# Two chunks of a state-space scan per visit to TensorE, between the products of an expert layer

## The chip, the cores and the metric

The kernel runs on one core of a Trainium2 chip. A core has five engines that run side by side and meet at semaphores: TensorE (PE in the profile, its weight loads PEld), VectorE (DVE), ScalarE (ACT), GpSimd (POOL) and SyncE (SP), which here only issues DMAs. The metric is the device time of one execution in microseconds. Before the change the median of three runs is 651.06 us (650.8 to 651.61).

## The reference

Two parts, the second of which reads the output of the first. The first is a Mamba-2 layer (4 sequences, 8 heads, 768 tokens, head size 32, state size 16), here cut to one chunk:

```python
cum = np.cumsum(la, axis=-1)                     # la: log of the decays a
L = np.exp(cum[..., :, None] - cum[..., None, :]) * causal
M = np.einsum('bhin,bhjn->bhij', Cc, Bc) * L
y = M @ xc + np.einsum('bhin,bhnd->bhid', Cc, state) * np.exp(cum)[..., None]
state = decay_full * state + sum_j(Bc_j, xc_j, decay_from_j)
```

The result does not depend on the length of a chunk; the kernel takes 128 tokens. The second part is a sum over four experts on the 3072 tokens, each with 256 inputs and 1024 hidden units:

```python
p = domain_probs / (domain_probs.sum(-1, keepdims=True) + 1e-09)
for e in range(4):
    out += p[:, e:e + 1] * (np.maximum(x @ w1[e], 0.0) @ w2[e])
```

Everything is float32.

## The kernel before

**Blocks and steps.** There are 24 chunks of 128 tokens. Four of them, the k-th chunk of each of the four sequences, make block k of 512 tokens (`CPB` is 4, `NBLK` is 6). A block goes through the experts in 8 steps (`SPB`), one for each half of each expert's hidden units, so there are 48 steps; step n is step r = n % 8 of block k = n // 8. Steps 0 and 1 are done in the prologue in the plain way, with 8 products of blocks instead of 7. From step 2 on a loop (L736 to L821) runs.

**A step.** Both products of a step are 2 x 2 block products made with seven multiplications each, of sums and differences. `fmul(n, i)` is multiplication i of the first product (f1 to f7 below), `smul(n - 1, i)` that of the second product of the step before (s1 to s7). Each is two matmuls of 128 x 128 by 256, which in float32 are four instructions of PE. The order on PE in a step is

```
f1 f2 s1 f6 s3 [outputs] f5 f7 s7 s5 f3 f4 s6 s2 [scores] s4
```

The results of f go into two PSUM banks, X (f1, f6, f7, f4) and Y (f2; f5, f3). ACT copies X after f1, f6 and f7 (`snap`, L459). DVE adds such a copy to Y (`total`, L464), applies relu and the gate (`gated`, L474; `gated 21` reads X itself, after f4) and makes four differences `hT1` to `hT4` (`diff`, L481), of which two come at the end of the step and two, in the list `late`, after the first total and gate of the next one. The second product gathers in four PSUM banks, acc0 to acc3, over a block; at the beginning of the next block (r = 0 and 1) `keep`, `combine` and `turned_out` take the result out of them, and `leave` stores it in steps 2 to 5.

**The chunks of the next block** are worked between these products, one at a time. The programs of a chunk c:

- `load_chunk` (L120): tokens `xb` (L106; four buffers), the decays spread over all partitions `ab` (L112; three buffers), and the decays per head `ah` (L118; three buffers), all issued by SP
- `masks` (L355): two ACT instructions that make `ctm`, C with the one or the other half of the heads set to zero
- `decay_part` 0 and 1 (L322): each a scan on DVE over half of the heads, which makes half of `LT`, the decays between all pairs of tokens (L346); after the second, POOL makes the last columns of `MT`, B weighted for the state (L351)
- `decay_part` 2: a scan on DVE, `dec` (L329), and on POOL `cts`, C weighted with it (L332)
- `scores` (L362): products of C and B on PE, four 32-row tiles of the array, one for each quarter of the partitions, each into a PSUM bank of its own; for the chunks in the loop two banks of the pool `att`, X and Y (L369)
- `masked` (L375): four DVE products of these with `LT`, into `MT` (L379)
- `outputs` (L383): on PE the carried state times `cts` (L392, full array), and on top of it `MT` times x in 32-column tiles (L398); ACT copies the y (L404) and the new sum for the state (L407) out of PSUM
- `carry` (L409): three short DVE instructions that update the state of the sequence

`scores` or `outputs` of one or more chunks, between products that use the full array, are called a visit below. The entry of chunk c (masks, scans, scores, masked products) stands in steps r = 0, 2, 4, 6, its exit (outputs) in the step after, its carry in the one after that. For the first block that is fed in the loop, chunk 4 enters in the prologue (L713 to L730).

**What sets the order.** The schedule is written by hand: each engine works its instructions in the order in which the program calls them, and waits are put in where a tile is read, written or its buffer reused. A pool's tile with `bufs=n` takes the buffer of the n-th tile of its tag before it. In the pool `att`, two buffers are the rule; `LT` has one, and each `hT` has two in the pool `ffn`. SP issues its DMAs in order as well: weights of step n + 2, gates, outputs, and the chunk loads. POOL, in the first block, also makes sums of weights (`sum_w1`, `sum_w2`) and stores them.

Of the kernel before, what the change touches and what calls it, by code (L numbers as in the profile page):

```python
# [8 lines left out]
FP32 = mybir.dt.float32  # L9
# [8 lines left out]
def kernel(  # L18
# [9 lines left out]
):  # L28

# [79 lines left out]
    def load_decays(c, queue):  # L109
        if c >= SPREAD:  # L110
            ab = load.tile([P, NH * P], FP32, tag="ab", name="ab")
            nc.sync.dma_start(  # L112
                out=ab, in_=acut_d[real(c)].rearrange(
                    "h s -> (h s)").partition_broadcast(P))
            st.setdefault(c, {})["ab"] = ab
        if c >= CPB:
            ah = st[c]["ah"] = load.tile([HN, P], FP32, tag="ah", name="ah")
            queue.dma_start(out=ah, in_=ac_d[real(c)].unsqueeze(1).to_broadcast([NH, N, P]))  # L118

    def load_chunk(c):  # L120
        load_tokens(c)
        load_decays(c, nc.sync)
# [199 lines left out]
    def decay_part(c, part):  # L322

        s = st[c]
        if part == 2:
            if c >= CPB:

                s["dec"] = dec = att.tile([HN, P], FP32, tag="dec", name="dec")
                nc.vector.tensor_tensor_scan(  # L329
                    out=dec, data0=s["ah"], data1=zeros, initial=1.0, op0=ALU.mult, op1=ALU.add)  # L330
                s["cts"] = cts = att.tile([HN, NT, P], FP32, tag="cts", name="cts")
                nc.gpsimd.tensor_mul(cts, s["ctm"], dec.unsqueeze(1).to_broadcast([HN, NT, P]))  # L332
            return
        half = NH * P // 2
        if part == 0:
            if c >= SPREAD:
                s["a"] = [s["ab"][:, :half], s["ab"][:, half:]]
            LT = att.tile([P, NH * P], FP32, tag="LT", name="LT", bufs=1)
            s["LT"] = LT.rearrange("p (h s) -> p h s", h=NH)

            s["MT"] = att.tile([P, NH, P + N], FP32, tag="MT", name="MT")

        LT, w = s["LT"].rearrange("p h s -> p (h s)"), s["a"][0].shape[1]
        n = half // w
        for i in range(n * part, n * part + n):
            nc.vector.tensor_tensor_scan(  # L346
                out=LT[:, i * w:i * w + w], data0=s["a"][i],
                data1=ident.rearrange("p h s -> p (h s)")[:, :w], initial=0.0,
                op0=ALU.mult, op1=ALU.add)
        if part == 1 and c < NCH - CPB:  # L350
            nc.gpsimd.tensor_mul(  # L351
                s["MT"][:, :, P:], s["xb"][:, OB:OB + HN].rearrange("p (h n) -> p h n", h=NH),
                s["LT"][:, :, P - 1:P].to_broadcast([P, NH, N]))

# [7 lines left out]
    def scores(c, homes):  # L362

        s = st[c]
        s["g"] = []
        for q, (pool, tag) in enumerate(homes):
            k = slice(32 * q, 32 * q + 32)
            g = pool.tile([P, NT, P], FP32, tag=tag, name="g")
            nc.tensor.matmul(  # L369
                out=g.rearrange("p t s -> p (t s)"), lhsT=s["xb"][k, OBT:OBT + P],  # L370
                rhs=s["ctm"][k].rearrange("p t s -> p (t s)"),
                start=True, stop=True, tile_position=(32 * q, 0))
            s["g"].append(g)

    def masked(c, qs):  # L375
        s = st[c]
        for q in qs:
            h = slice(NT * q, NT * q + NT)
            nc.vector.tensor_mul(s["MT"][:, h, 0:P], s["g"][q], s["LT"][:, h])  # L379

    state = {}

    def outputs(c, pool, tag):  # L383

        s = st[c]
        k, i = divmod(c, CPB)
        first = k == 0
        w = P + N if k < NBLK - 1 else P
        xb, MT = s["xb"], s["MT"]
        y = pool.tile([P, NT, P + N], FP32, tag=tag, name="y")  # L390
        if not first:
            nc.tensor.matmul(  # L392
                out=y[:, :, 0:P], lhsT=state[i][1].rearrange("p q d -> p (q d)"),
                rhs=s["cts"], start=True, stop=False, skip_group_check=True)
        for t in range(NT):
            for q in range(NQ):
                h = NQ * t + q
                nc.tensor.matmul(  # L398
                    out=y[32 * q:32 * q + 32, t, 0:w], lhsT=xb[:, h * D:h * D + D],
                    rhs=MT[:, NT * q + t, 0:w], start=(first and t == 0), stop=True,  # L400
                    tile_position=(0, 32 * q), skip_group_check=True)
        if i == 0:
            yT[k] = ffn.tile([P, NT, BLK], FP32, tag="yT", name="yT")
        nc.scalar.copy(out=yT[k][:, :, i * P:i * P + P], in_=y[:, :, 0:P])  # L404
        if w > P:
            s["A"] = att.tile([P, NT, N], FP32, tag="A", name="A", bufs=4)
            nc.scalar.copy(out=s["A"], in_=y[:, :, P:])  # L407
# [70 lines left out]
    def diff(n, o, x, y):  # L478
        h = hid[n]
        h[o] = ffn.tile([P, JJ, HB], FP32, tag="h" + o, name="h" + o)  # L480
# [179 lines left out]
    scores(0, homes)  # L660
# [5 lines left out]
    masked(0, range(NQ))  # L666
    outputs(0, ps_att, "att")
    scores(1, banks)
# [4 lines left out]
    masked(1, range(NQ))  # L673
    outputs(1, ps_att, "att")
    spread(2, (1,))
    sum_w1(0, 0)
    load_decays(3, nc.sync)
# [6 lines left out]
    scores(2, homes)  # L684
# [8 lines left out]
    masked(2, range(NQ))  # L693
    outputs(2, ps_att, "att")

    scores(3, ((ps_s, "acc0"), (ps_s, "acc1"), (ps_s, "acc2"), (ps_att, "att")))
# [7 lines left out]
    masked(3, range(NQ))  # L704
    sum_w2(1, 0)
    plain_gated(1, 1)
    outputs(3, ps_att, "att")
# [5 lines left out]
    masks(4)  # L713
# [7 lines left out]
    decay_part(4, 2)  # L721
# [7 lines left out]
    scores(4, ((ps_att, "att"), (ps_att, "att"), (ps_f, "X"), (ps_f, "Y")))  # L729
    masked(4, (2, 3, 0, 1))  # L730
# [4 lines left out]
    late = []  # L735
    for n in range(PLAIN, NS):  # L736
        k, r = divmod(n, SPB)

        enter, exit = ({2: 1, 4: 2, 6: 3}, {2: 0, 3: 1, 5: 2, 7: 3}) if k == 0 else (
            {0: 0, 2: 1, 4: 2, 6: 3}, {1: 0, 3: 1, 5: 2, 7: 3})  # L740
        c_in, c_out = (CPB * (k + 1) + d[r] if r in d and k < NBLK - 1 else None
                       for d in (enter, exit))
# [15 lines left out]
        if c_in is not None:  # L758
            masks(c_in)
            decay_part(c_in, 0)  # L760
# [8 lines left out]
        if c_out is not None:  # L769
            outputs(c_out, ps_att, "att")  # L770
# [11 lines left out]
        if c_in is not None:  # L782
            decay_part(c_in, 1)
# [6 lines left out]
        if c_out is not None and c_out + 2 < NCH:  # L790
            load_chunk(c_out + 2)
# [7 lines left out]
        smul(n - 1, 6)  # L799
        smul(n - 1, 2)  # L800
        if c_in is not None:
            scores(c_in, ((ps_att, "att"), (ps_att, "att"), (ps_f, "X"), (ps_f, "Y")))
            masked(c_in, (2, 3, 0, 1))
        diff(n, "T3", "22", "12")
        if c_in is not None:
            decay_part(c_in, 2)
# [11 lines left out]
        if PLAIN < n <= CPB:  # L818
            late.append(lambda n=n: carry(n - 1))
        if c_out is not None:  # L820
            late.append(lambda c=c_out: carry(c))  # L821
# [48 lines left out]
```

## Time and profile before

| | |
|---|---|
| median of three runs | 651.06 us |
| the profiled execution | 650.64 us |
| its span, first to last instruction | 648.8 us |
| granted TensorE clock | 0.999 |
| POOL busy up to 105 us of the span (prologue and first block) | 65.9 us |
| POOL busy in the 544 us after | 43.2 us |
| matmuls of L369 (scores) | 192, 17.4 us in all |
| matmuls of L392 and L398 (outputs) | 40 and 384, 11.9 and 16.7 us in all |

The busy time of the table is that of one execution under the profiler. A line of a timeline gives the start from the beginning of the span, the length, the engine, the line of the kernel, the operation with what it writes and reads, how many instructions were merged into it, and in brackets how long the engine stood idle before it and what ended that. "Issue" stands where the engine waited for nothing that the profile shows. A wait line gives the total, the number of times and the longest.

### The profile page before, as it was taken

The page shows a single profiled execution, that of the slowest core. Times are in us where ns is not written, and L with a number is a line of the kernel's source. Part 1 is how long each engine was busy: PE and PEld are TensorE (multiplying, and loading weights), DVE is VectorE, ACT ScalarE, POOL GpSimd, SP SyncE. Part 2 cuts the span into 40 slices and gives each one's busy share as a digit, 9 for nine tenths or more (in the row PEclk, how much of TensorE's full clock was granted, in tenths as well). Part 3 has the DMA queues.
Part 4 walks back from the last instruction along what each step waited for, and adds up shares of the span by engine and source line. Part 5 has one row for each costly group of instructions (what it writes and reads, how often), then busy time and mean ns, then how long its engine had stood idle before and what let it go on. Part 6 is the DMA issues. An engine that isn't in the chain of part 4 may idle for free.

```text
span 648.8 us, 9091 instructions
## 1 busy us (share of the span) xinstructions
PE 643.4 (99%) x3367; PEld 541.9 (84%) x3367; DVE 478.4 (74%) x809; ACT 115.7 (18%) x247; POOL 109.2 (17%) x157
## 2 busy tenths in 40 slices
PE   9999999999999999999999999999999999999997
PEld 5888888888888888888888888888888888888886
DVE  7868878878677797686787867778767667756555
ACT  3011121211211122112121121122111211111110
POOL 4787565020000001000002000000100000100000
PEclk9999999999999999999999999999999999999999
DMA  6987977624678361777742467836185644156001
GB/s 226 331 292 250 341 285 244 228 108 130 200 244 302 124 233 32 241 225 251 242 153 91 131 204 218 323 135 223 38 250 171 241 178 129 60 161 226 1 0 33
DMA packets 95648, 121.61 MB, mean 187 GB/s; under 512 B 28520, under 2 KB 77556, under 8 KB 95604
## 3 DMA queue, kind: packets, MB, share of 16 engines
q1 hardware_dynamic: 92776, 111.20, 52.7%
q0 software_dynamic: 2304, 9.44, 3.6%
q8 instruction: 27, 0.44, 0.3%
q10 hardware_dynamic: 524, 0.39, 0.2%
q14 instruction: 17, 0.14, 0.1%
HBM read 108.16 MB, written 12.83 MB: 186 GB/s over the span
## 4 chain that ended last, share of the span: by engine, by line
PE 99%; DVE 0%; ACT 0%; issue 0%
PE acc L537 43%; PE X L452 24%; PE Y L452 19%; PE g L369 2%; PE y L398 2%; PE acc L518 2%; PE y L392 1%; PE X L501 1%; PE Y L501 1%; PE t L652 1%; PE a L312 1%; PE a L304 0%; PE gp L281 0%; PE turned L588 0%; DVE u L603 0%; DVE o L614 0%
## 5 line engine op out<-in xcount | busy, mean ns | idle before, releaser
L464 DVE TENSOR_TENSOR z<-Y,snap 128x512 f32<-128x512 f32 x138 | 94.7, 686 | 127.3 <-ACT snap L459 81.5
L537 PE MATMUL acc<-hT,wt 128*128 128x256 f32 x736 | 183.2, 382 | 0.0
L459 ACT COPY snap<-X 128x512 f32<-128x512 f32 x138 | 80.8, 586 | 465.8 <-PE X L452 465.8
L537 PEld LDWEIGHTS acc<-hT,wt 128*128 128x128 f32 x736 | 138.5, 190 | 23.7 <-issue 6.0
L452 PE MATMUL X<-yS,wt 128*128 128x256 f32 x552 | 141.8, 379 | 0.0
L537 PE MATMUL acc<-h,wt 128*128 128x256 f32 x552 | 141.6, 379 | 0.0
L452 PEld LDWEIGHTS X<-yS,wt 128*128 128x128 f32 x552 | 105.1, 190 | 14.1
L537 PEld LDWEIGHTS acc<-h,wt 128*128 128x128 f32 x552 | 105.1, 190 | 14.1
L474 DVE SCALAR_TENSOR_TENSOR h<-z,gate 128x512 f32<-128x512 f32 x138 | 97.8, 709 | 3.5 <-PE acc L518 0.4
L452 PE MATMUL Y<-yT,wt 128*128 128x256 f32 x368 | 94.5, 379 | 0.0
L452 PEld LDWEIGHTS Y<-yT,wt 128*128 128x128 f32 x368 | 68.9, 190 | 10.5 <-DVE z L464 0.2
L481 DVE TENSOR_TENSOR hT<-h,hT 128x512 f32<-128x512 f32 x92 | 66.3, 720 | 1.6
L481 DVE TENSOR_TENSOR hT<-h,h 128x512 f32<-128x512 f32 x92 | 61.5, 693 | 0.8
L346 DVE TENSOR_TENSOR_SCAN LT<-ab,ident 128x512 f32<-128x512 f32 x42 | 51.5, 1229 | 0.0
L351 POOL TENSOR_TENSOR MT<-xb,LT 128x128 f32<-128x128 f32 x20 | 8.2, 411 | 248.5 <-PE Y L452 120.4
L452 PE MATMUL Y<-yS,wt 128*128 128x256 f32 x184 | 49.3, 391 | 0.0
L452 PE MATMUL X<-yT,wt 128*128 128x256 f32 x184 | 47.2, 379 | 0.0
L379 DVE TENSOR_TENSOR MT<-g,LT 128x256 f32<-128x256 f32 x96 | 33.9, 416 | 17.9 <-PE g L369 17.9
L332 POOL TENSOR_TENSOR cts<-ctm,dec 128x256 f32<-128x256 f32 x20 | 20.0, 998 | 154.2 <-ACT snap L459 147.2
L452 PEld LDWEIGHTS Y<-yS,wt 128*128 128x128 f32 x184 | 33.4, 190 | 8.0 <-issue 4.2
L474 DVE SCALAR_TENSOR_TENSOR h<-X,gate 128x512 f32<-128x512 f32 x50 | 34.3, 686 | 6.4 <-PE X L452 4.2
L452 PEld LDWEIGHTS X<-yT,wt 128*128 128x128 f32 x184 | 35.0, 190 | 4.7
(94 smaller groups left out, 332.7 us busy)
## 6 DMA issues: line engine op xcount, KB each, us to landing
wt<-in_w_dram SPq DMA_DIRECT2D x112, 256.0 KB, 7.0
wt<-w_d SPq DMA_DIRECT2D x40, 640.0 KB, 4.9
wt<-w_d SPq DMA_DIRECT2D x40, 512.0 KB, 5.5
ab<-acut_d SPq DMA_DIRECT2D x21, 512.0 KB, 4.6
xb<-in_xbc_dram SPq DMA_DIRECT2D x24, 320.0 KB, 7.0
gate<-p_d SPq DMA_DIRECT2D x23, 256.0 KB, 7.8
w_d<-wt POOLq DMA_DIRECT2D x8, 640.0 KB, 6.2
wt<-in_w_dram SPq DMA_DIRECT2D x40, 128.0 KB, 2.5
```

The lines of the kernel that those rows point to most:

```text
L332: nc.gpsimd.tensor_mul(cts, s["ctm"], dec.unsqueeze(1).to_broadcast([HN, NT, P]))
L346: nc.vector.tensor_tensor_scan(out=LT[:, i * w:i * w + w], data0=s["a"][i], data1=ident.rearrange("p h s -> p (h s)")[:, :w], initial=0.0, ...
L369: nc.tensor.matmul(out=g.rearrange("p t s -> p (t s)"), lhsT=s["xb"][k, OBT:OBT + P], rhs=s["ctm"][k].rearrange("p t s -> p (t s)"), start ...
L379: nc.vector.tensor_mul(s["MT"][:, h, 0:P], s["g"][q], s["LT"][:, h])
L398: nc.tensor.matmul(out=y[32 * q:32 * q + 32, t, 0:w], lhsT=xb[:, h * D:h * D + D], rhs=MT[:, NT * q + t, 0:w], start=(first and t == 0), s ...
L452: nc.tensor.matmul(out=f[bank][:, j], lhsT=wt1[n][:, w, j * P:j * P + P], rhs=rhs, start=(i in (1, 2, 5) and j == 0), stop=(j == JJ - 1), ...
L459: nc.scalar.copy(out=s, in_=first[n]["X"])
L464: nc.vector.tensor_add(z, first[n]["Y"], first[n][i])
L474: nc.vector.scalar_tensor_tensor(out=h, in0=first[n][src], scalar=0.0, in1=g.unsqueeze(1).to_broadcast([P, JJ, HB]), op0=ALU.max, op1=ALU. ...
L481: nc.vector.tensor_sub(h[o], h[x], h[y])
L501: nc.tensor.matmul(out=f[bank][:, j], lhsT=wt1[n][:, w, j * P:j * P + P], rhs=yT[k][:, i, cols], start=(i == 0 and j == 0), stop=(i == 1), ...
L537: nc.tensor.matmul(out=acc[k, u][:, half], lhsT=w2_op(n, w)[:, j], rhs=rhs[:, j], start=(begins and j == 0), stop=(n % SPB == SPB - 1 and ...
```

## The change

The chunks of the next block are worked two by two on PE:

- The LT scans of a chunk (`decay_part` 0 and 1) stand in steps r = 0, 2, 4 and 5, one chunk in each.
- In steps 3 and 6 two chunks have their masks, their `dec` scans and `cts` (after `gated 22` now, no longer at the end of the step), their scores and their masked products. `scores` takes a list of chunks: the four banks are allocated once, each holds both chunks, and the eight float32 products stand one chunk after the other. It comes before s2 now; tile 2 goes into Y and tile 3 into X, and the masked products begin with X, then Y, both chunks of a bank together.
- In steps 4 and 7 two chunks have their outputs: both carried products, then the column tiles of both, then the copies.
- Carries are done one per step, in the two steps after the outputs. The first block's carries 2 and 3 come one step earlier.
- Chunk 4 loses its masks, `dec`, scores and masked products in the prologue to step 3.
- `LT` has two buffers, `ah` four, each `hT` one. `ab` of chunk c + 2 is loaded in the step of the scans of c, `xb` and `ah` of chunk c + 4 in the step of the outputs of c. The chunks 6 and 7 are still loaded whole, in steps 2 and 3.

```diff
-    def load_decays(c, queue):
...
+    def load_heads(c):
+        ah = st[c]["ah"] = load.tile([HN, P], FP32, tag="ah", name="ah", bufs=4)
+        nc.sync.dma_start(out=ah, in_=ac_d[real(c)].unsqueeze(1).to_broadcast([NH, N, P]))
...
-            LT = att.tile([P, NH * P], FP32, tag="LT", name="LT", bufs=1)
+            LT = att.tile([P, NH * P], FP32, tag="LT", name="LT")
...
+    def scores(cs, homes):
+        for c in cs:
+            st[c]["g"] = []
+        for pool, tag in homes:
+            g = pool.tile([P, len(cs), NT, P], FP32, tag=tag, name="g")
+            for j, c in enumerate(cs):
+                st[c]["g"].append(g[:, j])
+        for j, c in enumerate(cs):
+            s = st[c]
+            for q in range(NQ):
+                k = slice(32 * q, 32 * q + 32)
+                nc.tensor.matmul(
+                    out=s["g"][q].rearrange("p t s -> p (t s)"), lhsT=s["xb"][k, OBT:OBT + P],
+                    rhs=s["ctm"][k].rearrange("p t s -> p (t s)"),
+                    start=(j == 0), stop=True, tile_position=(32 * q, 0),
+                    skip_group_check=True)
+
+    def masked(cs, qs):
+        for q in qs:
+            h = slice(NT * q, NT * q + NT)
+            for c in cs:
+                s = st[c]
+                nc.vector.tensor_mul(s["MT"][:, h, 0:P], s["g"][q], s["LT"][:, h])
...
+    def outputs(cs):
+        ys = {}
+        for c in cs:
...
+                nc.tensor.matmul(
+                    out=y[:, :, 0:P], lhsT=state[i][1].rearrange("p q d -> p (q d)"),
+                    rhs=st[c]["cts"], start=True, stop=False, skip_group_check=True)
+        for c in cs:
...
+            for t in range(NT):
+                for q in range(NQ):
...
-        h[o] = ffn.tile([P, JJ, HB], FP32, tag="h" + o, name="h" + o)
+        h[o] = ffn.tile([P, JJ, HB], FP32, tag="h" + o, name="h" + o, bufs=1)
...
-    masks(4)
...
-    decay_part(4, 2)
...
-    scores(4, ((ps_att, "att"), (ps_att, "att"), (ps_f, "X"), (ps_f, "Y")))
-    masked(4, (2, 3, 0, 1))
...
+    states = [2, 3]
...
-        enter, exit = ({2: 1, 4: 2, 6: 3}, {2: 0, 3: 1, 5: 2, 7: 3}) if k == 0 else (
-            {0: 0, 2: 1, 4: 2, 6: 3}, {1: 0, 3: 1, 5: 2, 7: 3})
...
+        ahead = CPB * (k + 1)
+        scanned = [ahead + d for d in {0: [0], 2: [1], 4: [2], 5: [3]}.get(r, [])]
+        scored = [ahead + d for d in {3: [0, 1], 6: [2, 3]}.get(r, [])]
+        done = [ahead + d for d in {4: [0, 1], 7: [2, 3]}.get(r, [])]
...
+        for c in scanned:
+            decay_part(c, 0)
+        for c in scored:
+            masks(c)
...
+        if done:
+            outputs(done)
+            states.extend(done)
...
+        for c in scanned:
+            decay_part(c, 1)
+        for c in scored:
+            decay_part(c, 2)
...
-        if c_out is not None and c_out + 2 < NCH:
-            load_chunk(c_out + 2)
+        if n < CPB:
+            load_chunk(n + CPB)
+        for c in scanned if n >= CPB else []:
+            if c + 2 < NCH:
+                load_decays(c + 2)
+        for c in done:
+            if c + CPB < NCH:
+                load_tokens(c + CPB)
+                load_heads(c + CPB)
...
         smul(n - 1, 6)
+        if scored:
+            scores(scored, ((ps_att, "att"), (ps_att, "att"), (ps_f, "Y"), (ps_f, "X")))
+            masked(scored, (3, 2, 0, 1))
         smul(n - 1, 2)
-        if c_in is not None:
-            scores(c_in, ((ps_att, "att"), (ps_att, "att"), (ps_f, "X"), (ps_f, "Y")))
-            masked(c_in, (2, 3, 0, 1))
         diff(n, "T3", "22", "12")
-        if c_in is not None:
-            decay_part(c_in, 2)
...
-        if PLAIN < n <= CPB:
-            late.append(lambda n=n: carry(n - 1))
-        if c_out is not None:
-            late.append(lambda c=c_out: carry(c))
+        if states:
+            late.append(lambda c=states.pop(0): carry(c))
```

## The prediction

> **What bounds the kernel now.** I read the page's engine line first, then the waits, then two timelines of the weight loads, because one engine owns the span.
>
> ```profile
> PE 643.4 (99%) x3367; PEld 541.9 (84%) x3367; DVE 478.4 (74%) x809; ACT 115.7 (18%) x247; POOL 109.2 (17%) x157
> ...
> PE 99%; DVE 0%; ACT 0%; issue 0%
> ```
>
> TensorE is 99% of the span and of the chain that ended last. Its clock row on the page is full, so there is no throttle to win back. The reader should distrust the 99%, though: matmul ends are modelled, and idle time can hide behind them. The weight loads show it. In the list of waits:
>
> ```profile
> PEld y L398 <- issue: 7.3, 22, 0.3
> ...
> PEld g L369 <- issue: 6.1, 19, 0.3
> PEld acc L537 <- issue: 6.0, 18, 0.3
> ...
> PEld Y L452 <- issue: 4.2, 19, 0.2
> ```
>
> Some 80 times the loader stands 0.2 to 0.3 us with nothing to wait for, each time just before or after the small matmuls of `scores` (L369) or `outputs` (L398). The PEld timeline places them:
>
> ```profile
> 314.19 0.84 PEld L537 LDWEIGHTS acc<-h,wt 128*128 128x128 f32 x4
> 315.35 0.31 PEld L369 LDWEIGHTS g<-ctm,xb 32*128 32x128 f32 x8 [0.33 <-issue]
> 316.00 0.73 PEld L537 LDWEIGHTS acc<-hT,wt 128*128 128x128 f32 x4 [0.33 <-issue]
> 316.75 0.84 PEld L452 LDWEIGHTS X<-yT,wt 128*128 128x128 f32 x4
> ...
> 321.07 0.41 PEld L392 LDWEIGHTS y<-cts,M 128*128 128x128 f32 x2
> 321.81 0.40 PEld L398 LDWEIGHTS y<-MT,xb 128*32 128x32 f32 x16 [0.33 <-issue]
> 322.44 0.73 PEld L452 LDWEIGHTS Y<-yS,wt 128*128 128x128 f32 x4 [0.23 <-issue]
> ```
>
> 316.75 opens step 23. Loads that open other steps, in the same timeline:
>
> ```profile
> 303.82 0.84 PEld L452 LDWEIGHTS X<-yT,wt 128*128 128x128 f32 x4
> ...
> 330.10 0.84 PEld L452 LDWEIGHTS X<-yT,wt 128*128 128x128 f32 x4
> ...
> 552.14 0.84 PEld L452 LDWEIGHTS X<-yT,wt 128*128 128x128 f32 x4
> ...
> 564.23 0.84 PEld L452 LDWEIGHTS X<-yT,wt 128*128 128x128 f32 x4
> ```
>
> A step without a visit (552.14 to 564.23, last block) is 12.09 us: 14 products of 4 matmuls, 56 x 0.2155 = 12.07. TensorE waits for nobody there. Step 22, with one scores visit, is 12.93; step 23, with one outputs visit, 13.35. So a scores visit costs 0.84 us, an outputs visit 1.255 (1.20 in the last fed block, whose matmuls have 128 columns), and all matching steps of blocks 1 to 4 agree within 0.01. In the steady state only the visits are movable.
>
> **What the Trainium skill says.** "TensorEngine Tiling", section Tiling Modes (Key Properties): changing the tiling mode, not just the tile, drains TensorE. The trace agrees: 0.33 us before the 32-row and 32-column loads, 0.33 and 0.23 on the way back. "TensorE: Matmul & The Clock Gate", Part 3 (The mechanism): tiles in different row groups run together, some 4 ns apart; in the trace four L369 matmuls start within 20 ns. "TensorEngine Tiling", Gotcha 1 (PSUM Pressure): different row tiles must not use one PSUM bank at the same time. The pair keeps each row tile in a bank of its own and puts both chunks there, so that need not serialize; no run yet shows two chunks in a visit.
>
> **The change part by part.** Before, chunks 4 to 23 make 20 scores visits and 20 outputs visits; after, 10 and 10.
>
> Scores. One visit's instruction starts: last full matmul 315.046, first group of four 315.355, second 315.675, first full matmul 316.000, next 316.320: intervals 0.309, 0.320, 0.325, 0.320 = 1.274, where four intervals of stream are 0.862. The switches cost 0.412, the rest is two groups of 0.215. A second chunk adds two groups. At stream pitch that is 0.431, so a pair costs 1.273 instead of 1.685: 0.412 saved. Bounds: if each added group needs the 0.32 seen between the first two, 0.20 is saved; above 0.412 nothing can be saved. I take 0.412, since in full mode too only the first interval after a switch is 0.32 and the following ones are 0.215. Ten pairs: 4.1 us.
>
> Outputs. L392 is two full matmuls, 0.431. The column groups start at 321.808, .956, 322.078, .200: 0.148, then 0.122 each. A second chunk adds 0.431 + 4 x 0.122 = 0.919 to 1.255: a pair is 2.174 instead of 2.510, 0.336 saved. Bounds: at 0.148 a group 0.23; all of the excess 0.336 is the most. Ten pairs: 3.4 us. Sum: 7.5 us, all on the path.
>
> The scores move ahead of s2. Their fourth tile needs bank X, freed when `gated 21` has read f4. In a plain stretch:
>
> ```profile
> 300.58 1.03 PE L452 MATMUL X<-yS,wt 128*128 128x256 f32 x4
> ...
> 301.65 0.69 DVE L474 SCALAR_TENSOR_TENSOR h<-X,gate 128x512 f32<-128x512 f32 x1 [0.17 <-PE X L452]
> ```
>
> The gate ends 301.65 + 0.69 - 300.58 = 1.76 after f4 began. The fourth tile starts after f4, s6 and the switch, 0.862 + 0.862 + 0.09 + 0.02 = 1.83. Before, s2 lay between as well, 0.86 of cover; now 0.07 is left, less about 0.05 of wake-up (a DVE end at 311.59 let a load go at 311.64). I take zero stall, bounds 0 and 0.25 per visit.
>
> Do the two `dec` scans ahead of it delay the gate? Times from the step's first matmul: `gated 22` makes room at 8.20 (312.24 in step 22); two scans at a pitch of 0.33 (0.42 each) let `total 6` begin at about 8.88, against 8.83 when f3 allows it; 0.61 to 0.73 later the gate may start, 9.49 to 9.61, before f4 allows it at 9.69. They lie in DVE's idle time, by 0.08.
>
> Masked products. Scores end about 11.56; eight at 0.355 run from 11.64 to 14.48, X going first, free after two (12.4) and Y after four (13.1). Next step's f1 wants X at 13.36 and f2 wants Y at 14.22: one us of slack each. `diff T3` and `T1` follow to about 2.4 of the next step, so its first total starts at 2.35 instead of 2.00. The reader of that is s1 a step later and f5, at 6.4 after the visit. No cost. The tight one, `total 7` before f3 (ends 0.05 before the load in step 22), has a step with neither a pair's products nor late work before it: the outputs visit lies ahead of it and gives DVE 2.17 us more.
>
> Scans move to steps 0, 2, 4, 5 of a block, at the places of the same half-scans before; they fit there with the carry (step 22: 308.70 to 310.65, total at 310.90). Step 1 now has carry, combine and turn-out without a visit: 7.3 + 0.75 + 1.7 + 1.2 = 11 us in 12.09, and s6 wants its accumulator at 9.5, freed at about 8.7. ACT: two pairs of masks, 1.4 us, between the snaps ending 1.64 and starting 3.65; four copies, about 1.0, between 6.0 and 7.0, before snap 7 at 8.4. POOL: `cts` twice, ready by 11 of the scored step, wanted at 4.3 of the next; behind them in step 6 wait sums of four operations, some 3.5 us, done 1.2 into step 7, wanted at 3.4. In steps 3 to 5 of the first block the same sums end a step ahead of use.
>
> SP. `load_tokens(c+4)` wants a buffer that outputs of this same step frees, so SP, which now runs about one step ahead (it issues step 23's loads at 304 to 309, in step 22), stands until 5.5 into that step. Behind it queue the second chunk's two loads, gate and the weights of step n+3: issued 2.6 steps before use, over 30 us, against 7 to 8 us to land. `ab` and `ah` are loaded three or more steps early. No cost; were this cover gone, each late weight would show up whole. `hT*` with one buffer: each diff writes after the product that read the old one, by at least the totals and gates of a step. `LT` with two buffers takes a wait away. In the prologue chunk 4's visit and 2 us of DVE work leave; the visit is counted above, the DVE work lay beside plain matmuls, so nothing (bounds 0 and 0.3 gained).
>
> Sum: 650.64 for the profiled execution (span 648.8 and 1.84 around it) less 7.5 = 643.1. The median of the runs is 0.42 higher: 643.6.
>
> **The rivals.** (a) Pairs stream less well, or X is a little late: 0.20 + 0.23 a pair is 4.3 us, 646.8; with the full gain but X 0.25 late, 646.1. For: the 0.07 of cover, and that no pair is in the trace. Against: pitches of four groups in L398.
> (b) Slower: `gated 21` comes so late in the paired steps that scores stand at bank X, and everything behind them in TensorE's order with them. Every 0.1 us is paid ten times. The gain of a pair, 0.75, is gone when the gate is 0.8 late; at 1.2 late the time is 651.1 - 7.5 + 11 = 655. It would need DVE held by something outside this sum, such as a scan waiting for `ah`, or the two scans finding POOL in their way. Against: `ah` is there steps before, and 0.7 of idle DVE lies before the gate.
> (c) The drains are paid per chunk and not per visit, since the second chunk reloads the same row groups: 651. Against: within one chunk the second pass reloads the same groups and pays 0.10, not 0.33.
>
> **How the numbers follow.** Forecast 643.6: 0.73, its own range 642.8 to 644.8. (a) 0.12, (c) 0.04, (b) 0.11. The range 642.5 to 648 takes in the forecast and (a), 0.85. About 0.2% is what a measurement here can tell from no change. Faster: the forecast and (a), 0.85; same 0.04; slower 0.11.
>
> **What would show it.** Right: steps 3 and 6 of a block near 13.36 us, steps 4 and 7 near 14.26, the others 12.09; issue waits of PEld at L369 and L398 about halved; L369 still waiting for no engine. Wrong: PEld L369 waiting for DVE h L474 (X late), a group pitch of 0.3 inside the pair, f1 or f2 waiting for L379, or a weight load waiting for a DMA.

## The result and the profile after

The changed kernel takes 645.11 us (median of four runs, 644.61 to 646.3) where the kernel before takes 650.93 on the same chip: a ratio of 0.9912, interval 0.9895 to 0.9929. Run again with another set it was 646.09 against 650.87, 0.9925 (0.991 to 0.994). So it is faster by 0.8%: 5.8 us between the medians of the first set, 4.8 in the second, and 5.4 between the two profiled executions (650.64 and 645.25), where the forecast had 7.5.

The page after, engine line and shares of the chain:

```profile
PE 636.3 (99%) x3367; PEld 544.7 (85%) x3367; DVE 483.9 (75%) x809; ACT 115.5 (18%) x247; POOL 108.3 (17%) x157
...
PE 96%; DVE 1%; DMA 1%; SPq 0%; ACT 0%; issue 0%; POOL 0%; ACTq 0%; DVEq 0%; POOLq 0%
```

TensorE has the same number of instructions and 7 us less busy time, but the chain is no longer its own alone: 1% of it now runs through DVE and 1% through a DMA, a load of `xb` in the prologue. The waits of PE and PEld say where (the line numbers are those of the changed kernel: L376 scores, L398 and L408 outputs, L465 the f products, L550 the s products, L477 `total`, L487 `gated`, L494 `diff`, L348 the scan):

```profile
PEld y L408 <- issue: 4.0, 12, 0.3
PEld g L376 <- issue: 3.8, 12, 0.3
...
PEld acc L550 <- issue: 3.0, 9, 0.3
PEld Y L465 <- issue: 2.0, 9, 0.2
PEld Y L465 <- DVE z L477: 1.9, 2, 1.6
...
PE Y L465 <- DVE z L477: 1.2, 1, 1.2
```

The stalls around the visits are halved (7.3 to 4.0, 6.1 to 3.8, 6.0 to 3.0, 4.2 to 2.0). Beside them stands a wait that was 0.2 us in the kernel before: twice in the execution the load of f3 waits for `total 7`, once 1.6 us long. In a steady step the pairs look like this in the PEld timeline:

```profile
310.80 0.74 PEld L376 LDWEIGHTS g<-ctm,xb 32*128 32x128 f32 x16 [0.33 <-issue]
...
317.81 0.84 PEld L398 LDWEIGHTS y<-cts,M 128*128 128x128 f32 x4
318.98 0.89 PEld L408 LDWEIGHTS y<-MT,xb 128*32 128x32 f32 x32 [0.33 <-issue]
320.10 0.73 PEld L465 LDWEIGHTS Y<-yS,wt 128*128 128x128 f32 x4 [0.23 <-issue]
```

Twice the instructions (x16, x32) behind one drain of 0.33. From the start of one step's first product to the next, in both traces, in us:

| step r of a block | 0 | 1 | 2 | 3 | 4 | 5 | 6 | 7 |
|---|---|---|---|---|---|---|---|---|
| before, blocks 1 to 3 | 12.93 | 13.34 | 12.93 | 13.34 | 12.93 | 13.34 | 12.93 | 13.34 |
| after, blocks 1 to 3 | 12.09 | 12.09 | 12.09 | 13.36 | 14.26 | 12.09 | 13.36 | 14.26 |
| before, block 0 | | | 15.20 | 13.34 | 12.97 | 13.34 | 12.93 | 13.34 |
| after, block 0 | | | 13.09 | 13.52 | 14.26 | 13.60 | 13.36 | 14.26 |

A pair of scores costs 13.36 - 12.09 = 1.27, forecast 1.273; a pair of outputs 14.265 - 12.087 = 2.18, forecast 2.174. Blocks 1 to 4 did what was forecast. The miss lies ahead of them: step 3 is 0.16 and step 5 is 1.51 longer than their kind, and the prologue ended 0.33 earlier (the loop's first product starts at 38.68 and not 39.02) instead of the 0.84 of the visit that left it, 0.51 short. The forecast for this execution was 650.64 - 7.48 = 643.16, and 643.16 + 0.16 + 1.51 + 0.51 = 645.34, against 645.25.

Step 5 of the first block in the timeline of the changed kernel:

```profile
82.28 1.45 DVE L487 SCALAR_TENSOR_TENSOR h<-z,gate 128x512 f32<-128x512 f32 x1
82.44 0.73 POOL L162 TENSOR_TENSOR wt<-wt 128x256 f32<-128x256 f32 x1
...
83.25 1.07 POOL L163 TENSOR_TENSOR wt<-wt 128x256 f32<-128x256 f32 x1
83.65 2.35 DVE L494 TENSOR_TENSOR hT<-h,hT 128x512 f32<-128x512 f32 x2
...
84.40 1.06 POOL L164 TENSOR_TENSOR wt<-wt 128x256 f32<-128x256 f32 x1
...
86.16 0.48 DVE L430 SCALAR_TENSOR_TENSOR S<-S,dec 128x32 f32<-128x32 f32 x1
...
86.88 1.22 DVE L348 TENSOR_TENSOR_SCAN LT<-ab,ident 128x512 f32<-128x512 f32 x1
...
88.02 0.66 DVE L477 TENSOR_TENSOR z<-Y,snap 128x512 f32<-128x512 f32 x1
88.72 0.69 DVE L487 SCALAR_TENSOR_TENSOR h<-z,gate 128x512 f32<-128x512 f32 x1
88.73 0.73 PEld L465 LDWEIGHTS Y<-yT,wt 128*128 128x128 f32 x4 [1.65 <-DVE z L477]
```

DVE never idles from 82.28 to 88.7, so its queue is what is late. But the gate takes 1.45 us at 82.28 and 0.69 at 88.72; two differences take 2.35, which in a steady step take 1.41; the carry's second instruction 0.48 and not 0.25. POOL makes weight sums (L162 to L166) beside all of these, until 86.59; the scan after that, at 86.88, takes its usual 1.22. Step 5 starts at 79.56, and in most steps without an outputs visit this total begins 6.86 after the start; so it should have begun at 86.42, and began 1.60 late.

### The profile page after: what moved, and what is told of

It reads as the page before. It is cut to its first block, busy times and chain, and to the rows that moved or that the text cites. A ratio compares the mean times of both kernels' runs of the same rounds, so it can differ in the third digit from the quotient of the medians.

```text
span 643.5 us, 9107 instructions
## 1 busy us (share of the span) xinstructions
PE 636.3 (99%) x3367; PEld 544.7 (85%) x3367; DVE 483.9 (75%) x809; ACT 115.5 (18%) x247; POOL 108.3 (17%) x157
## 3 DMA queue, kind: packets, MB, share of 16 engines
HBM read 108.16 MB, written 12.83 MB: 188 GB/s over the span
## 4 chain that ended last, share of the span: by engine, by line
PE 96%; DVE 1%; DMA 1%; SPq 0%; ACT 0%; issue 0%; POOL 0%; ACTq 0%; DVEq 0%; POOLq 0%
PE acc L550 43%; PE X L465 24%; PE Y L465 19%; PE acc L531 2%; PE y L408 2%; PE g L376 2%; PE y L398 1%; PE X L514 1%; PE Y L514 1%; DMA xb<-in_xbc_dram 1%; DVE hT L494 0%; DVE h L487 0%; DVE z L477 0%; DVE LT L348 0%; SPq L134 0%
## 5 line engine op out<-in xcount | busy, mean ns | idle before, releaser
L477 DVE TENSOR_TENSOR z<-Y,snap 128x512 f32<-128x512 f32 x138 | 94.5, 685 | 127.5 <-ACT snap L472 76.4
L550 PE MATMUL acc<-hT,wt 128*128 128x256 f32 x736 | 181.3, 379 | 0.0
L550 PEld LDWEIGHTS acc<-hT,wt 128*128 128x128 f32 x736 | 140.0, 190 | 18.8
L550 PE MATMUL acc<-h,wt 128*128 128x256 f32 x552 | 142.6, 381 | 0.0
L465 PE MATMUL X<-yS,wt 128*128 128x256 f32 x552 | 141.8, 379 | 0.0
L550 PEld LDWEIGHTS acc<-h,wt 128*128 128x128 f32 x552 | 104.2, 190 | 16.9 <-issue 3.0
L465 PEld LDWEIGHTS X<-yS,wt 128*128 128x128 f32 x552 | 105.0, 190 | 14.3 <-issue 0.3
L487 DVE SCALAR_TENSOR_TENSOR h<-z,gate 128x512 f32<-128x512 f32 x138 | 100.1, 725 | 3.5 <-PE acc L531 0.4
L465 PE MATMUL Y<-yT,wt 128*128 128x256 f32 x368 | 94.7, 380 | 1.2 <-DVE z L477 1.2
L465 PEld LDWEIGHTS Y<-yT,wt 128*128 128x128 f32 x368 | 68.8, 190 | 12.3 <-DVE z L477 1.9
L494 DVE TENSOR_TENSOR hT<-h,hT 128x512 f32<-128x512 f32 x92 | 65.2, 709 | 1.8
L494 DVE TENSOR_TENSOR hT<-h,h 128x512 f32<-128x512 f32 x92 | 65.6, 754 | 1.1
L348 DVE TENSOR_TENSOR_SCAN LT<-ab,ident 128x512 f32<-128x512 f32 x42 | 52.1, 1242 | 0.0
L465 PE MATMUL Y<-yS,wt 128*128 128x256 f32 x184 | 48.3, 385 | 0.0
L465 PE MATMUL X<-yT,wt 128*128 128x256 f32 x184 | 47.3, 379 | 0.0
L465 PEld LDWEIGHTS Y<-yS,wt 128*128 128x128 f32 x184 | 34.2, 190 | 6.4 <-issue 2.0
L465 PEld LDWEIGHTS X<-yT,wt 128*128 128x128 f32 x184 | 35.0, 190 | 4.7
L487 DVE SCALAR_TENSOR_TENSOR h<-X,gate 128x512 f32<-128x512 f32 x50 | 34.2, 685 | 5.9 <-PE X L465 3.6
L334 POOL TENSOR_TENSOR cts<-ctm,dec 128x256 f32<-128x256 f32 x20 | 14.1, 726 | 133.9 <-DVE dec L331 133.9
```

The source lines that it names most:

```text
L348: nc.vector.tensor_tensor_scan(out=LT[:, i * w:i * w + w], data0=s["a"][i], data1=ident.rearrange("p h s -> p (h s)")[:, :w], initial=0.0, ...
L465: nc.tensor.matmul(out=f[bank][:, j], lhsT=wt1[n][:, w, j * P:j * P + P], rhs=rhs, start=(i in (1, 2, 5) and j == 0), stop=(j == JJ - 1), ...
L477: nc.vector.tensor_add(z, first[n]["Y"], first[n][i])
L487: nc.vector.scalar_tensor_tensor(out=h, in0=first[n][src], scalar=0.0, in1=g.unsqueeze(1).to_broadcast([P, JJ, HB]), op0=ALU.max, op1=ALU. ...
L494: nc.vector.tensor_sub(h[o], h[x], h[y])
L550: nc.tensor.matmul(out=acc[k, u][:, half], lhsT=w2_op(n, w)[:, j], rhs=rhs[:, j], start=(begins and j == 0), stop=(n % SPB == SPB - 1 and ...
```

## The experiments

**Theory.** A visit costs the mode changes of the array, from full-array products to 32-row or 32-column tiles and back, so a pair saves one set of them; and what was not gained is DVE being stretched by POOL's sums in the first block. **Rivals.** For the gain: fewer interruptions of the big products, whatever is inside a visit. For the shortfall: carry and scan in one half step are too much for DVE alone; or bank X, of which the forecast left 0.07 us of cover. Each kernel below is the changed kernel with one edit.

**outputs_by_chunk** puts each chunk's carried product before its own tiles:

```diff
 def outputs(cs):
     for c in cs:
...
-            if k > 0:
-                nc.tensor.matmul(
-                    out=y[:, :, 0:P], lhsT=state[i][1].rearrange("p q d -> p (q d)"),
-                    rhs=st[c]["cts"], start=True, stop=False, skip_group_check=True)
     for c in cs:
...
+            if k > 0:
+                nc.tensor.matmul(
+                    out=y[:, :, 0:P], lhsT=state[i][1].rearrange("p q d -> p (q d)"),
+                    rhs=st[c]["cts"], start=True, stop=False, skip_group_check=True)
             for t in range(NT):
```

> The same visits as in the changed kernel, but inside an outputs visit each chunk's carried product stands just before its own column tiles, so that the array changes its mode four times and not twice. If the mode changes are what a visit costs (theory), steps 4 and 7 of a block go from 14.26 back to 12.09 + 2 x 1.255 = 14.60 us (last fed block 14.49), and the whole from 645.1 to 648.5. If the gain came from fewer interruptions of the products around a visit, whatever is inside it (rival), these steps stay at 14.26 and the time at 645.1.

648.35 us (647.81 to 648.44). Steps 4 and 7 are 14.60 in every block of 144 columns and 14.49 in the last fed one, just as two single visits would be, and the loader's issue waits before L408 are again 7.3 us in 22 times, as in the kernel before. The same number of visits and the same neighbours, and the gain of the outputs is gone: it is the mode changes.

**scores_by_chunk** moves the second chunk's scores, and the masked products of both, behind s2 (`HOMES` stands for the four banks as in the change; the last argument says which chunks of the pair are worked):

```diff
         smul(n - 1, 6)
         if scored:
-            scores(scored, HOMES)
+            scores(scored, HOMES, (0,))
+        smul(n - 1, 2)
+        if scored:
+            scores(scored, HOMES, (1,))
             masked(scored, (3, 2, 0, 1))
-        smul(n - 1, 2)
```

> The scores of the pair's second chunk are moved behind the product s2, so that a full-array product lies between the two chunks; DVE and POOL do the same as in the changed kernel, their masked products start some 1.3 us later. If the mode changes cost 0.41 a time, steps 3 and 6 go from 13.36 to 13.77 us, the whole to 649.2; a little more if the later masked products free bank X too late for f1 (they free it about 0.05 us ahead). Rival, no price of the modes: 13.36 and 645.1.

650.64 us (649.57 to 652.79, twelve runs). Steps 3 and 6 are 13.80, and steps 4 and 7 14.34. The first is the forecast 0.41 and 0.03 more, the second 0.075 more than in the changed kernel; both extras come back in scores_late below, where they are read. Over ten pairs they make 1.0 of the 1.4 us by which the whole lies above the expected 649.2. With this and the run before, undoing either half loses its half: 0.44 and 0.34 a pair.

**sums_later** moves POOL's `sum_w2(5)` from the end of step 4 to the middle of step 5:

```diff
-        elif n == SPB - 2:
+        elif n in (SPB - 3, SPB - 2):
             sum_w2(n)
...
-        if PLAIN < n != SPB - 3:
+        if PLAIN < n and n not in (SPB - 4, SPB - 3):
             sum_w2(n + 1)
```

> The weight sums that POOL makes in the first half of step 5 of the first block (82.4 to 86.9 in the changed kernel) are issued in the middle of that step, behind the last columns of MT. Theory: DVE's gate, differences and carry in step 5 were stretched by POOL reading SBUF at the same time (gate 1.45 for 0.69, two differences 2.35 for 1.41), so total 7 came 1.6 late and f3 waited. Then step 5 goes from 13.60 to 12.09 to 12.2 us and the whole from 645.1 to 643.7. Rival: carry and scan in one half step are too much for DVE by themselves; then step 5 stays at 13.4 or more and the whole at 645.

643.53 us (643.47 to 644.02), ratio 0.9877 (0.986 to 0.9894). Step 5 is 12.09. From the loop's first product to the end it is 1.1 us shorter than the changed kernel; the rest of the difference lies in the prologue. Its DVE timeline, the same instructions as in step 5 above:

```profile
81.66 0.69 DVE L487 SCALAR_TENSOR_TENSOR h<-z,gate 128x512 f32<-128x512 f32 x1
82.27 1.41 DVE L494 TENSOR_TENSOR hT<-h,hT 128x512 f32<-128x512 f32 x2
...
83.83 0.25 DVE L430 SCALAR_TENSOR_TENSOR S<-S,dec 128x32 f32<-128x32 f32 x1
...
84.33 1.22 DVE L348 TENSOR_TENSOR_SCAN LT<-ab,ident 128x512 f32<-128x512 f32 x1
85.80 0.69 DVE L477 TENSOR_TENSOR z<-Y,snap 128x512 f32<-128x512 f32 x1 [0.25 <-ACT snap L472]
```

Carry and scan are both there, and DVE waits 0.25 us for the snap again, as in step 22 of the kernel before. The rival that they are too much by themselves falls. What I had not foreseen: the sums now reach further into step 6, which has a carry too, and it grows from 13.36 to 13.76.

**carries_later** leaves POOL alone and keeps the carries out of steps 3 and 5:

```diff
-        if states:
-            late.append(lambda c=states.pop(0): carry(c))
+        for _ in range({2: 0, 3: 2, 4: 0, 5: 2}.get(n, 1)):
+            if states:
+                late.append(lambda c=states.pop(0): carry(c))
```

> POOL as in the changed kernel; no carry in steps 3 and 5 of the first block, two in step 4 and two in step 6. If DVE's queue ahead of total 7 sets the stall, step 3 loses its 0.16 (13.36), and step 5 keeps what POOL's stretching of gate and differences costs, 1.6 less the carry's 0.97, some 0.6: 12.65 to 12.75 us. Together 1.0 to 1.1 gained, 644.0, unless two carries in step 6 are stretched in their turn (up to 0.5 lost there). Rival, that the carry has no part in it: 13.60 and 645.1.

644.0 us (643.86 to 645.75). Step 3 is 13.36 and step 6, with two carries, 13.36. But step 5 is 13.17, not 12.7. Its timeline tells why:

```profile
84.45 1.18 POOL L166 TENSOR_TENSOR wt<-wt 128x256 f32<-128x256 f32 x1
...
84.96 1.74 DVE L348 TENSOR_TENSOR_SCAN LT<-ab,ident 128x512 f32<-128x512 f32 x1
```

Without the carry the scan starts 0.95 us earlier against the step and meets POOL's last sum, so it is stretched in its turn, by 0.52. Taking work out of DVE's queue gave back less than its length. That the whole met the expected 644.0 is luck: the loop is only 0.6 us shorter than the changed kernel's and not 1.0, and the prologue of the profiled execution happened to end 0.8 earlier (37.87 and not 38.68).

**pool_reads** puts POOL work where there was none, in the first half of step 5 of blocks 1 to 4, and **pool_writes** the same with memsets after one addition:

```diff
+    scratch = const.tile([P, HB], FP32, name="scratch")
...
         gated(n, "11", "z11")
+        if r == 5 and 0 < k < NBLK - 1:
+            for _ in range(6):
+                nc.gpsimd.tensor_add(scratch, hid[n]["11"][:, 0], ident01)
```

> In step 5 of blocks 1 to 4 POOL makes six additions of 128 x 256 from SBUF into a scratch tile that nobody reads, from when gate 11 is done (3.4 us into the step); the rest is the changed kernel. Theory: two differences, the carry and the scan before total 7 take 2.35 + 0.97 + 1.74 us and not 1.41 + 0.75 + 1.22, total 7 comes about 1.4 late, and these four steps go from 12.09 to about 13.5, the whole to 650.6. Rival, only the traffic of weights and sums in the first block makes DVE slow: 12.09 and 645.1.

> As pool_reads, but POOL makes one addition and then twelve memsets of the same scratch tile, so that it writes SBUF and reads none of it while DVE works through the differences, the carry and the scan. If only POOL's reads hold DVE up (the Trainium skill, SBUF - State Buffer, on the shared port pair), the stretch is that of one addition, 0.3 to 0.5 us, and steps 13, 21 and 29 (12.83, 13.23 and 12.83 in pool_reads) stay below 12.3; the whole at 645.1 to 645.5. If any work of POOL does it, they are as in pool_reads and the whole at 647.4.

Here `ident01` is two of the identity blocks as one operand; in pool_writes the addition stands once and is followed by twelve `nc.gpsimd.memset(scratch, 0.0)`. Step 13 in the timelines, pool_reads first:

```profile
187.65 1.82 DVE L494 TENSOR_TENSOR hT<-h,hT 128x512 f32<-128x512 f32 x2
187.81 6.74 POOL L768 TENSOR_TENSOR scratch<-h,ident 128x256 f32<-128x256 f32 x6 [5.62 <-DVE h L487]
189.62 0.48 DVE L430 SCALAR_TENSOR_TENSOR S<-S,dec 128x32 f32<-128x32 f32 x1
190.34 1.75 DVE L348 TENSOR_TENSOR_SCAN LT<-ab,ident 128x512 f32<-128x512 f32 x1
192.02 0.66 DVE L477 TENSOR_TENSOR z<-Y,snap 128x512 f32<-128x512 f32 x1
192.73 0.73 PEld L465 LDWEIGHTS Y<-yT,wt 128*128 128x128 f32 x4 [0.88 <-DVE z L477]
```

```profile
188.33 1.81 DVE L494 TENSOR_TENSOR hT<-h,hT 128x512 f32<-128x512 f32 x2
188.49 1.11 POOL L767 TENSOR_TENSOR scratch<-h,ident 128x256 f32<-128x256 f32 x1 [5.62 <-DVE h L487]
189.66 4.37 POOL L769 MEMSET scratch<- 128x256 f32 x12
190.30 0.25 DVE L430 SCALAR_TENSOR_TENSOR S<-S,dec 128x32 f32<-128x32 f32 x1
190.80 1.22 DVE L348 TENSOR_TENSOR_SCAN LT<-ab,ident 128x512 f32<-128x512 f32 x1
191.93 0.66 DVE L477 TENSOR_TENSOR z<-Y,snap 128x512 f32<-128x512 f32 x1
```

With reads, the carry's 0.25 becomes 0.48 and the scan's 1.22 becomes 1.75, and f3 waits for the total: steps 13, 21 and 29 are 12.83, 13.23 and 12.83, the whole 647.43 (647.12 to 647.61). With writes, the same DVE instructions at the same place keep their lengths; only the differences beside the one addition are stretched, 1.41 to 1.81. Steps 13 and 29 are 12.09, the whole 645.67 (644.86 to 646.15). Two misses in size: I expected 1.4 us in four steps of pool_reads, and it was 0.75 to 1.14 in three, because the first difference had begun before POOL did (it took 0.68, its usual time, and only the second was stretched, to 1.10) and, it seems, because the last fed block's carries do nothing (step 37 stayed 12.09). And step 21 of pool_writes was 12.43 where I said below 12.3: in step 21 the first total begins 0.34 later than in other steps, in the changed kernel too, and it had that much less idle time to spend. The trace does not say why. The whole of pool_writes, 645.67, lies 0.2 above the range that I gave; step 21 alone added 0.34.

**scores_early** and **scores_late** move scores and masked products by one product, to before s6 or to after s2:

```diff
+        if scored:
+            scores(scored, HOMES)
+            masked(scored, (3, 2, 0, 1))
         smul(n - 1, 6)
-        if scored:
-            scores(scored, HOMES)
-            masked(scored, (3, 2, 0, 1))
         smul(n - 1, 2)
```

```diff
         smul(n - 1, 6)
-        if scored:
-            scores(scored, HOMES)
-            masked(scored, (3, 2, 0, 1))
         smul(n - 1, 2)
+        if scored:
+            scores(scored, HOMES)
+            masked(scored, (3, 2, 0, 1))
```

> Scores and masked products one product earlier, before s6 and not after it. The fourth tile then wants bank X 0.97 us after f4 began, and the gate that frees X ends 1.76 after it. If the bank is what holds the place of the scores (the slower case of the forecast), each pair stalls 0.8 to 0.9 us, steps 3 and 6 go from 13.36 to 14.2, and the whole to 653.5, slower than the kernel before. If PE went on with the other tiles and products meanwhile, or the bank were free earlier than reckoned, 13.4 and 645.

> Scores and masked products one product later, after s2, as in the kernel before. Bank X has been free for 0.9 us, so if the changed kernel stalls there by a little that the step times hide, steps 3 and 6 fall below 13.36. If its cover of 0.07 is just enough, as forecast, they do not. On the other side the masked products end 0.86 later: X is freed at about 13.3 and wanted by f1 at 13.36, Y at 14.0 and 14.2; 13.36 to 13.45 a step, 645.1 to 646.

scores_early takes 653.52 us (652.83 to 654.8), ratio 1.0038 (1.0027 to 1.005): slower than the kernel before. Its PEld timeline of one pair:

```profile
314.46 0.31 PEld L376 LDWEIGHTS g<-ctm,xb 32*128 32x128 f32 x6 [0.33 <-issue]
315.31 0.72 PEld L376 LDWEIGHTS g<-ctm,xb 32*128 32x128 f32 x10 [0.55 <-DVE h L487]
316.37 0.73 PEld L550 LDWEIGHTS acc<-hT,wt 128*128 128x128 f32 x4 [0.33 <-issue]
```

Six loads go, then the fourth tile's waits for the gate that reads X, and all behind it with it (ten loads). Steps 3 and 6 are 14.19, 0.83 more than in the changed kernel. scores_late takes 645.78 us (645.37 to 646.05): steps 3 and 6 are 13.39 and steps 4 and 7 14.34, 0.03 and 0.075 more. Here f1 of the next step waits: its load stands 0.24 before it goes, since the second of the eight masked products (273.34 to 276.08), the last that reads X, ends only at 274.10. f1's first matmul starts 0.03 late, at 274.20, and its second another 0.075, which falls into the next step. So the slot of the change has almost no room on the early side, where one product (0.86) costs 0.83, and some 0.7 us on the late side, where one product costs 0.1: in the changed kernel the second masked product of step 22 ends at 312.77 and f1's load goes at 313.50. No step shows it stalling on either side.

**both_moved** joins what helped. The sums as in sums_later, two carries in step 4, and none in steps 3 and 6; `dec` gets a third buffer, so that chunk 5's carry may stand in step 7:

```diff
+        for _ in range({2: 0, 3: 2, 5: 0}.get(n, 1)):
+            if states:
+                late.append(lambda c=states.pop(0): carry(c))
...
-    dec = att.tile([HN, P], FP32, tag="dec", name="dec")
+    dec = att.tile([HN, P], FP32, tag="dec", name="dec", bufs=3)
```

> The sums of step 5 later, as in sums_later, and the carries kept out of the steps in which POOL makes sums while total 7 is near: none in steps 3 and 6 of the first block, two in step 4, chunk 4's in step 5, chunk 5's in step 7 (dec has three buffers for that). Theory, POOL reading SBUF beside DVE's two-input instructions is what is left: steps 3, 5 and 6 at 13.36, 12.09 and 13.36 (13.55, 12.09 and 13.76 in sums_later), the whole 0.6 below sums_later: 642.9, and no wait of PE for DVE in the loop. Rival, something else in the first block holds DVE as well: a rest of 0.2 or more in steps 3 to 6.

643.36 us (642.94 to 644.69), ratio 0.9886 (0.987 to 0.9901). Steps 3, 5 and 6 of the first block are 13.36, 12.09 and 13.36, and PE waits for DVE nowhere in the loop; the total is 0.2 under sums_later rather than 0.6. In the profiled executions the prologue ended 0.26 later, which accounts for the difference there; the two also ran on different chips, on which the kernel before took 651.93 and 650.81, so that the medians can't tell them apart and the step lengths have to. The interval of its ratio lies clear of that of the changed kernel's second set and overlaps a little with that of the first.

**changed_again** is the changed kernel, unedited:

> The changed kernel once more, nothing edited, for the spread of the prologue. If the 0.5 us that the prologue fell short in the first profile came from when the first loads landed, the loop's first product starts at another time here (37.9 to 39.0 us) while every step of the loop has the same length within 0.1, and steps 3 and 5 stall again, at 13.5 and 13.6. If it belonged to the change, the start is 38.7 again. 645.1 in all, within 0.6.

646.09 us (644.94 to 646.35). The loop starts at 39.76, and every step of it has its former length within 0.01 (13.52 and 13.59 for steps 3 and 5). So the prologue varies and the loop does not; but by more than I expected, since 39.76 lies outside 37.9 to 39.0 and the whole is 1.0 above 645.1. The prologue is the same program in all kernels from the changed one on; the loop started at 38.68, 38.40, 39.87, 38.03, 37.87, 38.29, 39.05, 38.45, 38.34, 39.02 and 39.76 in their profiles.

Two causes can be read from the traces. One is a load of `xb`, issued at the same 4.75 us before and after the change. ACT's third mask waits for it, the copy of `p_sb` stands behind that mask in ACT's queue, and TensorE waits for the copy. In the first profile of the changed kernel:

```profile
10.90 0.69 ACT L362 ACTIVATE ctm<-xb,tmask 128x128 f32<-128x128 f32 x2 [3.21 <-DMA xb<-in_xbc_dram]
...
12.14 1.05 PE L283 MATMUL gp<-p_sb,ident 96*128 96x128 f32 x7 [0.56 <-ACT p_sb L274]
```

In the profile of the kernel before, the mask began at 10.24 and TensorE was busy throughout these microseconds; so these 0.56 us account for the 0.51 that the prologue fell short. In the other traces the mask began anywhere from 9.46 to 11.89. The other cause shows in the two latest starts, scores_by_chunk and changed_again: there the eight matmuls of L314 from about 7.9 us on take 3.2 us where they take 2.0 in the first profile. An estimate for all runs on record, not only the profiled ones: subtract from each time the 1.8 us around the span and what its kernel's trace has from the loop's first product to the end. The loop then starts at a median of 39.3 us in the 36 runs of the kernel before, and of 38.4 in the 55 runs of the changed kernel and its variants, 0.9 earlier. That agrees with the 0.84 of the forecast, and the first pair of profiles showed less of it than the runs as a whole.

## Why the prediction was right, and where it was short

**Direction and mechanism: right, the size by luck.** 645.1 lies in the stated range of 642.5 to 648, but 1.5 above the forecast of 643.6 and outside the forecast's own 642.8 to 644.8. The range holds it only because it was drawn wide enough for rival (a), and what rival (a) says did not happen: the 1.5 came from a term that the sum had put at nothing (below).

**The saving per pair: right.** 0.41 for scores and 0.33 for outputs, forecast 0.412 and 0.336. The added groups run at stream pitch, as taken and not at the 0.32 of the lower bound; rivals (a), in its first form, and (c) are out; the second form of (a), X late, falls with the next point.

**Bank X: right, and rightly feared.** Zero stall in the changed kernel: its wait list has no wait of L376 for a gate. One product earlier the stall is 0.83, from the forecast's own numbers 0.84 (1.76 + 0.05 - 0.97); at that place the mechanism of rival (b) alone made the kernel slower than before. It did not hold here.

**Masked products, masks, copies, SP, weights: right.** No step of blocks 1 to 4 is longer than its products and visits. SP does stand, as foreseen, for the outputs to free a buffer (eight waits for L408, 91.7 us in all), and no step is longer for it.

**The step that failed** is the one on the scans and carries. It put "at the places of the same half-scans before; they fit there with the carry" on step 22 as its model, and of POOL it asked only whether "the same sums end a step ahead of use". They do. But in the first block DVE does not have step 22's durations while POOL sums: the 0.25 us between scan and `total 7` was nearly all the cover there was, and DVE came 1.60 late in step 5. In the kernel before, such a step had no scan: DVE stood idle ahead of its total for 3.35 us in the steady state (step 21) and still for 1.18 in step 5 itself. Likewise the carries of the first block that come one step earlier, costed at nothing with the rest, cost 0.16 in step 3. Together 1.67 of the shortfall of the profiled execution; the other 0.51 is the prologue, which varies from run to run. Between the medians the stalls alone account for it: 643.6 + 1.67 = 645.3, against 645.1. I gave rival (b) the words "the two scans finding POOL in their way", but meant the `dec` scans before `gated 21`; the place was another one, `total 7`, and the price a single step's.

The trace of before had it:

```profile
42.27 1.05 POOL L162 TENSOR_TENSOR wt<-wt 128x256 f32<-128x256 f32 x1
42.66 1.74 DVE L346 TENSOR_TENSOR_SCAN LT<-ab,ident 128x512 f32<-128x512 f32 x1
43.28 1.64 POOL L164 TENSOR_TENSOR wt<-wt 128x256 f32<-128x256 f32 x1
```

A scan that starts inside one POOL sum takes 1.74, and the sum that starts inside the scan takes 1.64, where the mean of L164 is 0.84. I took medians by line, and a median of 1.22 hides it. The Trainium skill says it too: "SBUF — State Buffer", section Who interferes with whom, has it that a DVE instruction with two SBUF inputs contends with a GpSimd instruction that reads SBUF, and not with one that only writes. pool_reads and pool_writes agree on both halves. That page says the later one blocks wholly until the first is done. The traces agree in the main: in carries_later the scan that starts 0.51 into a POOL sum (84.96 against 84.45) grows by 0.52, where 0.67 of that sum were left by its recorded length, and in pool_reads the first addition, which starts 0.16 after a difference, takes 1.11 while that difference keeps its 0.68. One pattern does not fit. In step 5 of the changed kernel the gate starts at 82.28, 0.16 before the sum at 82.44, and it is the gate that takes twice its time, 1.45, while the sum takes the 0.73 that it takes alone. The same shows in carries_later (81.31) and sums_later (93.75), and each time POOL was issuing a DMA when the gate began. Whether that decides the order is not shown.

**Open.** Why step 21's first total is late; why the load of `xb` lands at such different times, and why TensorE's first matmuls take longer in two of the traces; and what decides which of DVE and POOL goes first when both start within 0.2 us, as at 82.28.

## What to carry to other kernels

Where TensorE is full, count its mode changes and not its small matmuls: put side by side what uses the same tiling, also across items, and price a visit from the starts of the instructions, drain in and drain out apart. When work moves to another step, its new neighbours on other engines count as well as its new place in its own queue: take durations from a stretch in which the same engines are busy. And know the cover on both sides of a slot that banks set; here one product earlier turns a gain of 5.4 us into a loss of 2.7.

## What the runs showed of the hardware that was not expected

- A DVE instruction that reads two operands from SBUF is stretched while POOL reads SBUF: gate 0.69 to 1.45, difference 0.69 to 1.1 or more, scan 1.22 to 1.74, the short update of the state 0.25 to 0.48. One that reads one operand from PSUM is not: `total` 0.66 to 0.69 beside POOL and alone. POOL is stretched as well: an addition of 128 x 256 takes 0.73 alone and, beside such instructions, 1.06 to 1.17 (1.52 and 1.64 beside a scan).
- POOL's memsets of 128 x 256, 0.36 us apart, did nothing to the carry and the scan beside them (0.25 and 1.22 in pool_writes).
- As the forecast had taken it, sixteen float32 row-tile matmuls in a visit run as four groups of four, the second 0.32 us after the first and the others at the pitch of full-array matmuls, 0.216 us (starts at 310.80, 311.12, 311.34 and 311.56), also where a second chunk's weights replace the first's in the same rows and its results go to the same four banks.
